# Sixteen output tensors, one for each batch and channel half, in place of one

## The chip, the cores and the metric

The kernel runs on one core of a Trainium2 chip. The metric is device time in microseconds (us), from the start to the end of one execution; less is better. A core has five engines with a queue each: PE (matrix multiply), DVE (vector), ACT (scalar), POOL (GpSimd) and SP, which issues transfers. An engine works its queue strictly in order. A transfer (DMA) runs on its own once it is issued; whoever needs its result, or the memory that it reads, waits on a semaphore that it raises when it has landed. Here SP issues all plain transfers and POOL all indirect ones (gathers and scatters of rows by a list of indices).

## What is computed

For each of 8 batches x[b] of 3136 tokens with 256 channels, the kernel filters along the tokens in the frequency domain. It then picks the 128 tokens with the largest score against a gate vector, and adds to these a gated feed-forward result; all other tokens stay as the filter left them.

```python
X = np.fft.rfft(x, axis=1)
y = np.fft.irfft(X * (filt_r + 1j * filt_i)[None], n=3136, axis=1)
scores = np.einsum('bsd,d->bs', y, w_gate)
out = y.copy()
for b in range(8):
    top = np.argpartition(-scores[b], 128)[:128]
    xe = y[b, top]
    ye = np.maximum(xe @ w1, 0.0) @ w2            # 256 -> 1024 -> 256
    out[b, top] = xe + sigmoid(scores[b, top])[:, None] * ye
```

## The kernel before

The filter of a batch is a transform of two factors (98 x 32), a product with the filter, and the way back. `outer` runs the first and last stage over 8 chunks of 32 channels: it takes batch b_out out and brings batch b_in in at the same time. `inner` does the middle stage. The way out of a chunk ends in matmuls (`imm`, L531), copies from PSUM by ACT into a tile `xh` and into `X` (`iout`, L537) and an addition and a subtraction by POOL or DVE (`join`, L541). `xh` has four buffers, so ACT's copy for a chunk waits until the joins four chunks earlier are done.

`X` holds one batch in two channel halves. When the four chunks of a half x are done, `store_rows` (L577, issued by SP) writes the half to the output in DRAM, 2 MB at a time: 16 stores in all. The output is one tensor, `out_0_dram`, of 8 batches x 8192 rows of 128 channels; rows 0 to 4095 of a batch are its first channel half, the next 4096 its second.

`select` finds the 128 tokens of a batch by counting against thresholds and ends in `c12`: it writes two columns of row numbers to `idx_sb`, one for each half (L867, L868). The number includes the batch's offset, which L637 adds. `ffn` then takes the batches in the groups [0], [1], [2, 3, 4], [5, 6] and [7]: `gather` (L962) fetches the 128 rows, one indirect DMA for each half; PE transposes them (L968), multiplies with w1 (L991 or L998) and w2 (L1026 or L1031); `gated` (L1034, DVE) adds the result to the gathered rows; `scatter` (L1039) writes them back, again one indirect DMA for each half. The batches 0 and 1 use the tile `xr`, the others rows of `fb_sb`.

The order of all instructions is fixed: the steps are recorded and run in the order of the list `ORDER`, so each engine's queue is written by hand. What an instruction waits for isn't written by hand. The framework finds it from the tiles and DRAM ranges that the instruction reads and writes, and places the waits. Gathers and scatters give it a range of the output, not rows, since the rows are known only at run time: `of[:(b + 1) * ROWS]`, the whole output from its start to the end of batch b. The DMAs that POOL issues take eight semaphores in turn (DMASW0 to DMASW7 in the rows below), so each also waits for the one that used its semaphore before, eight issues earlier.

## Time and profile before

| | us |
|---|---|
| median of 3 runs | 461.66 (460.04 to 465.23) |
| the profiled execution | 465.2 |
| its span, first to last instruction | 463.4 |

| engine | busy us | share of the span |
|---|---|---|
| PE | 412.6 | 89% |
| DVE | 362.4 | 78% |
| POOL | 344.1 | 74% |
| ACT | 313.4 | 68% |

The profile gives, for one execution, when each instruction ran, how long its engine sat idle just before it, and which event ended that idle time. The releaser is inferred from semaphores: where an instruction waits for several, the one named is the one that came last by the profile, and a name that had long been done stands for another, often a DMA. A DMA that POOL issues shows as busy time of POOL while its descriptors are made; the data lands later. PEclk is the granted clock of PE as a share of full speed, 2.4 GHz; its lower level is 1.2 GHz.

### The profile page before, as it was taken

Reading aid. Unit: us, or ns where it says so; the run is one execution under the profiler, and the core shown is the slowest. Engines: PE = TensorE matmul, PEld = TensorE weight load, DVE = VectorE, ACT = ScalarE, POOL = GpSimd, SP = SyncE. Lnnn points to the kernel's source line nnn. Section 1 sums busy time; section 2 is a strip of 40 time slices with the busy share of each in tenths; the row PEclk is TensorE's granted clock in tenths of the full one; section 3 lists DMA queues with packets and bytes.
Section 4 is the critical chain, followed back from the end, with each engine's and each line's share of the span. In section 5 each row is a group of like instructions: output and inputs, shape, how many; then the busy total and the mean of one; then the engine's idle time right before and its main releaser. Section 6 shows DMA issues by size and latency. Waiting matters only on the chain.

```text
span 463.4 us, 13106 instructions
## 1 busy us (share of the span) xinstructions
PE 412.6 (89%) x5348; PEld 246.1 (53%) x5348; DVE 362.4 (78%) x727; ACT 313.4 (68%) x798; POOL 344.1 (74%) x231
## 2 busy tenths in 40 slices
PE   9999999999799999998999999999999895988710
PEld 9645555445545554465545444554567552877700
DVE  3668999989888989996799999989999984552300
ACT  1719866997578898877797977799899774421100
POOL 3218989799797968899989884998899959452332
PEclk9999999999899999999999999999999997999965
DMA  8899441174627464555445466424264340441000
GB/s 286 269 327 345 178 185 38 70 296 185 219 92 274 182 219 192 199 190 213 182 184 223 180 230 272 168 101 180 95 229 181 119 194 23 171 154 63 24 23 23
DMA packets 12554, 80.82 MB, mean 174 GB/s; under 512 B 3150, under 2 KB 6222, under 8 KB 7886
## 3 DMA queue, kind: packets, MB, share of 16 engines
q1 hardware_dynamic: 11470, 77.89, 44.9%
q0 software_dynamic: 1024, 2.10, 1.5%
q8 instruction: 42, 0.69, 0.6%
q14 instruction: 18, 0.15, 0.1%
HBM read 45.20 MB, written 34.78 MB: 173 GB/s over the span
## 4 chain that ended last, share of the span: by engine, by line
PE 39%; DVE 28%; ACT 12%; POOL 9%; issue 8%; DMA 3%; POOLq 0%; ACTq 0%; DVEq 0%
DVE t L479 6%; DVE UU L505 5%; DVE y L384 5%; ACT junk L441 5%; DVE q L391 4%; PE pv L998 3%; PE py L500 3%; DMA out_dram<-fb_sb,idx_sb 3%; PE pa L500 3%; PE pv L500 2%; POOL q L435 2%; PE py L400 2%; PE pa L376 2%; ACT junk L716 2%; PE pv L400 2%
## 5 line engine op out<-in xcount | busy, mean ns | idle before, releaser
L435 POOL TENSOR_TENSOR q<-UU,wg_sb 128x1024 f32<-128x1024 f32 (+1 forms) x47 | 110.2, 2352 | 12.7 <-ACT UU L408 6.3
L541 POOL TENSOR_TENSOR X<-xh,X 113x512 f32<-113x512 f32 x64 | 82.0, 1292 | 13.4 <-ACT X L537 9.4
L441 ACT ACTIVATE junk<-q 128x256 bf16<-128x256 f32 x180 | 75.1, 417 | 11.4 <-POOL q L435 6.5
L479 DVE STREAM_TRANSPOSE t<-UU 128x1024 f32<-128x1024 f32 x64 | 78.0, 1223 | 0.0
L387 POOL TENSOR_TENSOR q<-q,fb_sb 128x1024 f32<-128x1024 f32 (+1 forms) x18 | 40.7, 2262 | 11.6 <-ACT q L380 11.5
L489 POOL TENSOR_TENSOR X<-X 113x512 f32<-113x512 f32 x24 | 31.3, 1307 | 15.5 <-DVE xh L489 7.6
L489 POOL TENSOR_TENSOR xh<-X 113x512 f32<-113x512 f32 x26 | 33.5, 1297 | 6.5 <-DMA X<-in_x_dram 6.5
L716 ACT ACTIVATE junk<-R,nb 128x392 bf16<-128x392 f32 (+1 forms) x48 | 30.0, 625 | 6.6 <-DVE nb L737 6.0
L441 ACT ACTIVATION_READ_ACCUMULATOR junk<-q 128x1 f32 x180 | 33.9, 188 | 0.0
L500 PE MATMUL pa<-X,c_sb 49*64 49x512 f32 x192 | 30.3, 596 | 0.7 <-DVE UU L505 0.5
L500 PE MATMUL pv<-X,c_sb 49*64 49x512 f32 x184 | 29.7, 612 | 0.0
L505 DVE STREAM_TRANSPOSE UU<-pa 128x1024 f32<-128x1024 f32 x21 | 25.9, 1232 | 4.9 <-PE pa L500 4.8
L1039 POOL DMA_INDIRECT out_dram<-fb_sb,idx_sb x12 | 11.7, 973 | 24.2 <-DMA out_dram<-fb_sb,idx_sb 19.2
L505 DVE STREAM_TRANSPOSE UU<-pv 128x1024 f32<-128x1024 f32 x19 | 23.4, 1233 | 5.5 <-PE pv L500 5.3
L1010 ACT ACTIVATE q<-pv 128x384 fp32r<-128x384 f32 (+2 forms) x18 | 8.0, 457 | 29.1 <-PE pv L998 20.5
L1012 DVE SCALAR_TENSOR_TENSOR y<-pv,q 128x384 fp32r<-128x384 f32 (+2 forms) x18 | 9.0, 511 | 23.1 <-ACT q L1010 18.5
L384 DVE TENSOR_TENSOR y<-pa,fa_sb 128x1024 f32<-128x1024 f32 (+1 forms) x19 | 22.5, 1185 | 3.7 <-PE pa L376 1.5
L500 PE MATMUL py<-X,c_sb 49*64 49x512 f32 x168 | 23.9, 592 | 0.0
L376 PE MATMUL pa<-UU,tf_sb 64*64 64x256 f32 x292 | 21.8, 406 | 1.6 <-ACT X L567 0.5
L563 PE MATMUL pz<-t,c_sb 64*64 64x512 f32 x160 | 22.2, 595 | 0.1
L400 PE MATMUL py<-y,ti_sb 64*64 64x256 f32 x252 | 21.1, 380 | 0.6 <-DVE y L384 0.6
L400 PE MATMUL py<-q,ti_sb 64*64 64x256 f32 x252 | 20.9, 376 | 0.0
(342 smaller groups left out, 1167.8 us busy)
## 6 DMA issues: line engine op xcount, KB each, us to landing
out_dram<-X SPq DMA_DIRECT2D x16, 2048.0 KB, 6.8
X<-in_x_dram SPq DMA_DIRECT2D x14, 2048.0 KB, 8.6
X<-in_x_dram SPq DMA_DIRECT2D x4, 1024.0 KB, 12.9
R<-scr SPq DMA_DIRECT2D x14, 196.0 KB, 3.4
fb_sb<-in_moe_w_dram SPq DMA_DIRECT2D x2, 1024.0 KB
fa_sb<-in_fri_dram SPq DMA_DIRECT2D x4, 256.0 KB, 8.7
fb_sb<-in_fri_dram SPq DMA_DIRECT2D x4, 256.0 KB
ti_sb<-in_ti_dram SPq DMA_DIRECT2D x1, 576.0 KB, 10.2
```

Of the source, the lines that this page charges most:

```text
L376: nc.tensor.matmul(z[o, hi, e], lhsT=tf_sb[p, l], rhs=urow(b, l, 0, D)[p], start=True, stop=True)
L384: nc.vector.tensor_tensor(out=wide(y), in0=wide(h["z"]), in1=filt(fa_sb), op=ALU.mult)
L387: nc.gpsimd.tensor_tensor(out=wide(h["q"]), in0=wide(h["q"]), in1=filt(fb_sb), op=ALU.mult)
L400: nc.tensor.matmul(v[o, j, c], lhsT=ti_at[p, k, 2 * i + e, hi], rhs=y[p, hi, c], start=k == 0, stop=k == 1)
L435: nc.gpsimd.tensor_tensor(out=h["q"][:, e0:e0 + ne].rearrange("p e (j d) -> p e j d", j=2), in0=u.rearrange("p e d j -> p e j d"), in1=wg_ ...
L441: nc.scalar.activation(out=rk, in_=h["q"][:, e, j * D:j * D + D], func=AF.Copy, accum_out=urow(b, ls[2 * e + j], D, DS))
L479: nc.vector.transpose(out=h["t"].rearrange("p d (l j) -> p d l j", j=2), in_=uchan(b_out, c))
L489: eng.tensor_tensor(out=(area(1) if k else h["f"])[:64 + NH], in0=area(0)[:64 + NH], in1=area(1)[:64 + NH], op=(ALU.add, ALU.subtract)[k])
L500: nc.tensor.matmul(ap[64 * k:64 * k + 64, g].rearrange("p (n d) -> p n d", d=DW), lhsT=todo[k][i][0][p], rhs=todo[k][i][1][p], start=i == ...
L505: nc.vector.transpose(out=uchan(b_in, c), in_=a.rearrange("p (l j) d -> p d l j", j=2))
L541: eng.tensor_tensor(out=area(k)[:64 + NH], in0=h["e"][:64 + NH], in1=odd, op=(ALU.add, ALU.subtract)[k])
L716: nc.scalar.activation(out=junk, in_=st["R"][:, ph], func=AF.Sign, bias=st["nb"], accum_out=cnt)
```

## The change

The output becomes 16 DRAM tensors of 4096 rows, `yd[b][x]`, one for each batch and channel half; in the program they are `out_0_dram` to `out_15_dram`, with batch b in 2b and 2b + 1. A token's row number is now the same in both halves and has no batch offset, so `idx_sb` has one column for each batch: L868 falls away, and the addition of L637 becomes a copy. Stores, gathers and scatters name their own tensor. The host puts the tensors together by a reshape, as it did before. `ORDER` is the same.

```diff
--- before.py
+++ after.py
-ROWS = 8192
+ROWS = 4096
...
-    cst: bass.AP, wg: bass.AP, w1: bass.AP, w2: bass.AP, out: bass.AP, C: int,
+    cst: bass.AP, wg: bass.AP, w1: bass.AP, w2: bass.AP, yd: list, C: int,
...
-    of = out.rearrange("b s d -> (b s) d")
...
-    idx_sb = const.tile([128, 2 * B], I32, name="idx_sb")
+    idx_sb = const.tile([128, B], I32, name="idx_sb")
...
     def store_rows(b, x):
-        to = out[b, 4096 * x:4096 * x + 4096].rearrange("(p r) d -> p (r d)", p=128)
-        nc.sync.dma_start(out=to, in_=X[:, x].rearrange("p k n d -> p (k n d)"))
+        nc.sync.dma_start(out=yd[b][x].rearrange("(p r) d -> p (r d)", p=128), in_=X[:, x].rearrange("p k n d -> p (k n d)"))
...
-            nc.vector.tensor_scalar(out=Dt[:, 2 * N2:], in0=cc["row"][:N1], scalar1=float(b * ROWS), scalar2=None, op0=ALU.add)
+            nc.vector.tensor_copy(out=Dt[:, 2 * N2:], in_=cc["row"][:N1])
...
-            st["idx"] = idx = idx_sb[:, 2 * b:2 * b + 2]
+            st["idx"] = idx = idx_sb[:, b:b + 1]
...
-            nc.vector.tensor_scalar(out=idx[:C, 1:], in0=idx[:C, :1], scalar1=4096.0, scalar2=None, op0=ALU.add)
...
         def gather(j):
             for x in range(2):
-                nc.gpsimd.indirect_dma_start(out=xe[j][:C, x * HD:x * HD + HD], out_offset=None, in_=of[:(bs[j] + 1) * ROWS],
-                                             in_offset=bass.IndirectOffsetOnAxis(ap=sts[bs[j]]["idx"][:C, x:x + 1], axis=0))
+                nc.gpsimd.indirect_dma_start(out=xe[j][:C, x * HD:x * HD + HD], out_offset=None, in_=yd[bs[j]][x],
+                                             in_offset=bass.IndirectOffsetOnAxis(ap=sts[bs[j]]["idx"][:C, 0:1], axis=0))
...
         def scatter(j):
             for x in range(2):
-                nc.gpsimd.indirect_dma_start(out=of[:(bs[j] + 1) * ROWS],
-                                             out_offset=bass.IndirectOffsetOnAxis(ap=sts[bs[j]]["idx"][:C, x:x + 1], axis=0),
+                nc.gpsimd.indirect_dma_start(out=yd[bs[j]][x],
+                                             out_offset=bass.IndirectOffsetOnAxis(ap=sts[bs[j]]["idx"][:C, 0:1], axis=0),
                                              in_=xe[j][:C, x * HD:x * HD + HD], in_offset=None)
...
-    args.append(nc.dram_tensor("out_0_dram", (B, ROWS, D // 2), F32, kind="ExternalOutput").ap())
+    yd = [[nc.dram_tensor(f"out_{2 * b + x}_dram", (ROWS, D // 2), F32, kind="ExternalOutput").ap() for x in range(2)] for b in range(B)]
+    args.append(yd)
```

The instructions of PE, ACT and SP stand as before. On DVE eight instructions (L868) are gone. On POOL every instruction stands at its place, but their waits differ. Three places follow; a row is a line of the code, the operation, output<-input with buffer numbers, the size, and the semaphores that the instruction waits for (DMASW: DMAs issued by POOL; DMAHW: by SP; else an engine). Lines of the change lie 2 or 3 below those of before (L1036 is L1039, L959 is L962, L540 is L541, L930 is L933).

POOL, where it scatters batch 0, before:

```order
L933 TENSOR_TENSOR fa_sb_4718<-fb_sb_88,fa_sb_4718 128x512
L1039 DMA out_0_dram<-xr_97,idx_sb_91 8192x128 [waits DMASW4_49,DMASW5_49,DMASW3_49,DMASW6_49,DMASW2_49,DMASW7_49,DMASW1_49,DMASW0_49]
L1039 DMA out_0_dram<-xr_97,idx_sb_91 8192x128 [waits DMASW2_49]
L933 TENSOR_TENSOR ti_sb_4819<-fb_sb_88,ti_sb_4819 128x512 [waits PE_49,Activation_49]
L933 TENSOR_TENSOR fa_sb_4718<-fb_sb_88,fa_sb_4718 128x512 [waits Activation_49]
L541 TENSOR_TENSOR X_89<-xh_4964,X_89 113x16x32 [waits DMAHW4_49]
L541 TENSOR_TENSOR X_89<-xh_5055,X_89 113x16x32 [waits Activation_49]
L541 TENSOR_TENSOR X_89<-xh_4964,X_89 113x16x32 [waits Pool_49]
```

The same place in the change:

```order
L930 TENSOR_TENSOR fa_sb_4713<-fb_sb_88,fa_sb_4713 128x512
L1036 DMA out_0_dram<-xr_97,idx_sb_91 4096x128 [waits DMASW2_49]
L1036 DMA out_1_dram<-xr_97,idx_sb_91 4096x128 [waits DMASW3_49]
L930 TENSOR_TENSOR ti_sb_4813<-fb_sb_88,ti_sb_4813 128x512 [waits PE_49,Activation_49]
L930 TENSOR_TENSOR fa_sb_4713<-fb_sb_88,fa_sb_4713 128x512 [waits Activation_49]
L540 TENSOR_TENSOR X_89<-xh_4958,X_89 113x16x32 [waits DMAHW4_49]
L540 TENSOR_TENSOR X_89<-xh_5049,X_89 113x16x32 [waits Activation_49]
L540 TENSOR_TENSOR X_89<-xh_4958,X_89 113x16x32 [waits Pool_49]
```

Before, the first scatter waits for all eight DMAs last issued, and the second for DMASW2, which is the first. In the change the two write two tensors and wait only for the DMAs that used DMASW2 and DMASW3 eight issues earlier, the gathers of batch 1.

POOL, where it gathers batch 7, before:

```order
L541 TENSOR_TENSOR X_89<-xh_5186,X_89 113x16x32
L541 TENSOR_TENSOR X_89<-xh_5186,X_89 113x16x32 [waits Pool_49]
L541 TENSOR_TENSOR X_89<-xh_5228,X_89 113x16x32
L962 DMA fb_sb_88<-out_0_dram,idx_sb_91 128x128 [waits DMAHW6_49,DMAHW7_49,DVE_49,PE_49]
L962 DMA fb_sb_88<-out_0_dram,idx_sb_91 128x128 [waits DVE_49,PE_49]
```

The same place in the change:

```order
L540 TENSOR_TENSOR X_89<-xh_5180,X_89 113x16x32
L540 TENSOR_TENSOR X_89<-xh_5180,X_89 113x16x32 [waits Pool_49]
L540 TENSOR_TENSOR X_89<-xh_5221,X_89 113x16x32
L959 DMA fb_sb_88<-out_14_dram,idx_sb_91 128x128 [waits DMASW2_49,DMAHW6_49,DVE_49,PE_49]
L959 DMA fb_sb_88<-out_15_dram,idx_sb_91 128x128 [waits DMAHW7_49,DMASW3_49,PE_49]
```

Before, the first of the two gathers carries the waits for both stores of batch 7; in the change each waits for the store of its own half, and for a semaphore last used by the scatters of batch 0.

The end of POOL's queue, the scatters of batches 2 to 7, before:

```order
L1039 DMA out_0_dram<-fb_sb_88,idx_sb_91 24576x128 [waits DMASW3_49,DMASW2_49,DMASW6_49,DMASW1_49,DMASW7_49,DMASW0_49,DVE_49]
L1039 DMA out_0_dram<-fb_sb_88,idx_sb_91 24576x128 [waits DMASW4_49]
L1039 DMA out_0_dram<-fb_sb_88,idx_sb_91 32768x128 [waits DMASW5_49,DVE_49]
L1039 DMA out_0_dram<-fb_sb_88,idx_sb_91 32768x128 [waits DMASW6_49]
L1039 DMA out_0_dram<-fb_sb_88,idx_sb_91 40960x128 [waits DMASW7_49,DVE_49]
L1039 DMA out_0_dram<-fb_sb_88,idx_sb_91 40960x128 [waits DMASW0_49]
L1039 DMA out_0_dram<-fb_sb_88,idx_sb_91 49152x128 [waits DMASW1_49,DVE_49]
L1039 DMA out_0_dram<-fb_sb_88,idx_sb_91 49152x128 [waits DMASW2_49]
L1039 DMA out_0_dram<-fb_sb_88,idx_sb_91 57344x128 [waits DMASW3_49,DVE_49]
L1039 DMA out_0_dram<-fb_sb_88,idx_sb_91 57344x128 [waits DMASW4_49]
L1039 DMA out_0_dram<-fb_sb_88,idx_sb_91 65536x128 [waits DMASW5_49,DVE_49]
L1039 DMA out_0_dram<-fb_sb_88,idx_sb_91 65536x128 [waits DMASW6_49]
```

The same place in the change:

```order
L1036 DMA out_4_dram<-fb_sb_88,idx_sb_91 4096x128 [waits DMASW4_49,DVE_49]
L1036 DMA out_5_dram<-fb_sb_88,idx_sb_91 4096x128 [waits DMASW5_49]
L1036 DMA out_6_dram<-fb_sb_88,idx_sb_91 4096x128 [waits DMASW6_49,DVE_49]
L1036 DMA out_7_dram<-fb_sb_88,idx_sb_91 4096x128 [waits DMASW7_49]
L1036 DMA out_8_dram<-fb_sb_88,idx_sb_91 4096x128 [waits DMASW0_49,DVE_49]
L1036 DMA out_9_dram<-fb_sb_88,idx_sb_91 4096x128 [waits DMASW1_49]
L1036 DMA out_10_dram<-fb_sb_88,idx_sb_91 4096x128 [waits DMASW2_49,DVE_49]
L1036 DMA out_11_dram<-fb_sb_88,idx_sb_91 4096x128 [waits DMASW3_49]
L1036 DMA out_12_dram<-fb_sb_88,idx_sb_91 4096x128 [waits DMASW4_49,DVE_49]
L1036 DMA out_13_dram<-fb_sb_88,idx_sb_91 4096x128 [waits DMASW5_49]
L1036 DMA out_14_dram<-fb_sb_88,idx_sb_91 4096x128 [waits DMASW6_49,DVE_49]
L1036 DMA out_15_dram<-fb_sb_88,idx_sb_91 4096x128 [waits DMASW7_49]
```

Before, the first waits for the gathers, and each further one for the DMASW of the scatter just ahead of it, beside DVE (`gated`) for the first half of a batch. In the change each waits for the DMA eight issues earlier, and for DVE in the same places.

## Rows read from the trace of the kernel before

**Rows 1.** Span of the core and its granted clock (us; 1.0 is full clock):
```profile
core 0: 463.4 us, clock 0.964
```

**Rows 2.** Page, costliest groups: busy us, mean ns | idle before, its releaser:
```profile
L1039 POOL DMA_INDIRECT out_dram<-fb_sb,idx_sb x12 | 11.7, 973 | 24.2 <-DMA out_dram<-fb_sb,idx_sb 19.2
```

**Rows 3.** Timeline of POOL at the end: start, us, instruction [idle before <-releaser]:
```profile
439.08 0.97 POOL L1039 DMA_INDIRECT out_dram<-fb_sb,idx_sb  x1 [2.15 <-DVE fb_sb L1034]
456.68 0.97 POOL L1039 DMA_INDIRECT out_dram<-fb_sb,idx_sb  x1 [2.14 <-DMA out_dram<-fb_sb,idx_sb]
459.42 0.97 POOL L1039 DMA_INDIRECT out_dram<-fb_sb,idx_sb  x1 [1.78 <-DMA out_dram<-fb_sb,idx_sb]
```

**Rows 4.** Timeline of DVE: the last results of the feed-forward batches:
```profile
418.46 0.47 DVE L1034 SCALAR_TENSOR_TENSOR fb_sb<-pa,g_sb,fb_sb 128x256 f32<-128x256 f32 x1
438.35 0.48 DVE L1034 SCALAR_TENSOR_TENSOR fb_sb<-py,g_sb,fb_sb 128x256 f32<-128x256 f32 x1
441.53 0.48 DVE L1034 SCALAR_TENSOR_TENSOR fb_sb<-pa,g_sb,fb_sb 128x256 f32<-128x256 f32 x1 [2.11 <-PE pa L1031]
```

**Rows 5.** Line L1039 (scatters): us from a DMA's issue to its landing:
```profile
DMA to landing us min/median/max: 2.2/2.2/6.7
```

**Rows 6.** Line L962 (gathers): the same:
```profile
DMA to landing us min/median/max: 2.5/3.1/8.9
```

**Rows 7.** Timeline of POOL, scatters of batches 0 and 1:
```profile
373.10 1.01 POOL L1039 DMA_INDIRECT out_dram<-xr,idx_sb  x1 [0.16 <-issue]
379.38 0.98 POOL L1039 DMA_INDIRECT out_dram<-xr,idx_sb  x1 [5.27 <-PE py L727]
400.10 0.97 POOL L1039 DMA_INDIRECT out_dram<-xr,idx_sb  x1 [6.24 <-DMA out_dram<-xr,idx_sb]
```

**Rows 8.** Chain that ended last: start us, us, what:
```profile
382.91 3.65 POOL X L541 x3
```

**Rows 9.** Timeline of ACT, and of PE, after that:
```profile
386.59 0.59 ACT L537 COPY xh<-py 113x512 f32<-113x512 f32 x1 [5.36 <-POOL X L541]
387.72 0.50 PE L849 MATMUL pa<-Dt,rows 64*64 64x65 f32 x8 [5.25 <-ACT X L537]
```

**Rows 10.** Windows: busy us (xcount) PE PEld DVE ACT POOL, PEclk, DMA share, GB/s:
```profile
382.40:387.70 5.30, 0.07 (x6) 0.00 (x0) 0.97 (x4) 1.11 (x3) 5.30 (x5) 0.85 0.00 0
387.70:393.90 6.20, 6.18 (x42) 3.19 (x46) 4.27 (x16) 4.11 (x10) 6.00 (x6) 0.58 0.11 42
442.10:463.40 21.30, 0.00 (x0) 0.00 (x0) 0.00 (x0) 0.00 (x0) 6.50 (x7) 0.55 0.06 22
```

**Rows 11.** Timeline of PE: equal groups of matmuls before and after its idle time:
```profile
379.96 1.04 PE L531 MATMUL py<-t,c_sb 64*64 64x512 f32 x8
388.21 1.98 PE L531 MATMUL py<-t,c_sb 64*64 64x512 f32 x8
380.93 1.32 PE L998 MATMUL pv<-fa_sb 128*128 128x384 f32 x6
390.12 2.29 PE L998 MATMUL pv<-fa_sb 128*128 128x384 f32 x6
```

**Rows 12.** Timeline of POOL, gathers of batch 7:
```profile
422.26 0.96 POOL L962 DMA_INDIRECT fb_sb<-out_dram,idx_sb  x1 [9.53 <-DMA out_dram<-X]
423.52 0.94 POOL L962 DMA_INDIRECT fb_sb<-out_dram,idx_sb  x1 [0.30 <-issue]
```

**Rows 13.** Timeline of PE's weight loads: first transposes of batch 7:
```profile
426.25 0.14 PEld L968 LDWEIGHTS pz<-c_sb,fb_sb 128*128 128x128 f32 x1 [0.27 <-DMA fb_sb<-out_dram,idx_sb]
```

**Rows 14.** Timeline of DVE: the second index of batch 7:
```profile
416.04 0.15 DVE L868 TENSOR_SCALAR idx_sb<-idx_sb 128x1 int32<-128x1 int32 x1
```

**Rows 15.** Page, DMA issues: count, KB each, median us to landing:
```profile
out_dram<-X SPq DMA_DIRECT2D x16, 2048.0 KB, 6.8
X<-in_x_dram SPq DMA_DIRECT2D x14, 2048.0 KB, 8.6
X<-in_x_dram SPq DMA_DIRECT2D x4, 1024.0 KB, 12.9
```

## What the change is predicted to do

> **What bounds the kernel now.** I read the page first: PE is busy for most of the span, DVE, POOL and ACT for two thirds to three quarters, so no engine is the bound alone, and what counts is which wait ends last in each stretch. The page's costliest groups show one large idle time that isn't PE's: POOL sat idle for 24.2 us ahead of the twelve scatters of the batches 2 to 7, 19.2 of them until a scatter had landed [rows 2]. The chain that ended last shows where this counts: at its end it goes from scatter to scatter, of which the last starts at 459.42 [rows 3]. The windows say the same: from 442.1 to the end at 463.4 PE, DVE and ACT do nothing, and POOL is busy for 6.5 of 21.3 us, the DMA engines for 6% [rows 1, 10].
>
> The timeline of POOL shows the pattern. A scatter keeps POOL busy for 0.97 us, then POOL waits 1.78 or 2.14 us for its landing, then comes the next [rows 3]; a scatter takes 2.2 us from issue to landing [rows 5]. The results had long been there: batch 4's was done at 418.93, batch 6's at 438.83, and the last, batch 7's, at 441.53 + 0.48 = 442.01 [rows 4], but the last scatter started at 459.42 [rows 3].
>
> The same wait stands twice further up, where the batches 0 and 1 are written. There the second scatter waited 5.27 and 6.24 us [rows 7]. The releaser of the first is given as a matmul of PE, but the order shows that this scatter waits for DMASW2 alone, the scatter before it, which had started at 373.10: 379.38 - 373.10 = 6.28 us, near the longest landing of a scatter, 6.7 [rows 5]. What stands behind it in POOL's queue is wanted elsewhere: two parts of the weight split (L933), then the joins of batch 7. The first three joins ran until 382.91 + 3.65 = 386.56 [rows 8]; ACT sat idle for 5.36 us until then, because its next copy needs the `xh` buffer that they free, and PE sat idle for 5.25 us behind ACT [rows 9]. After that idle time the granted clock of PE was 0.58 over 387.7 to 393.9, so for the most part at the lower of its two levels, 1.2 in place of 2.4 GHz [rows 10]. Equal groups of matmuls took 1.98 in place of 1.04 us and 2.29 in place of 1.32 [rows 11].
>
> **The change part by part.** The waits between scatters, and between scatters and gathers, go. By the order each scatter now waits for DVE's result and for the DMA eight issues earlier. That one is long over: for batch 7's scatters it is batch 3's.
>
> *The end.* Batch 7's first scatter starts about 0.25 us behind its result, as batch 4's did behind a result that ended at 438.83 (439.08 - 438.83) [rows 3, 4]; so 442.01 + 0.25 = 442.26. The second follows at the step of two indirect DMAs that don't wait for each other, 423.52 - 422.26 = 1.26 us [rows 12]: 443.52. Before it was 459.42, so with the same end behind it the span is shorter by 15.9 us. For this POOL has to be through with the batches 2 to 6. It is free from 424.46 on, when batch 7's gathers are issued [rows 12], and batch 4's result is there by then. The eight scatters of 2 to 5 take 8 x 1.26 = 10.1 us of the 14.4 until batch 6's result at 438.83, and batch 6's pair is issued by 438.83 + 0.25 + 1.26 + 0.97 = 441.3 [rows 3, 4, 12], ahead of batch 7's. POOL's issuing isn't the bound.
>
> No row shows two scatters in flight. The nearest is gathers in a row, 2.5 to 3.1 us to landing [rows 6] against 2.2 [rows 5]; the last scatter lands between 0 and 0.9 us later than now. I take 0, since the last pair runs with nothing else in flight. At the far end stands the 6.7 us of [rows 5], which is a rival below. The Trainium skill, page "DMA: Bandwidth & Descriptors", section "Rules for kernel authors", speaks against splitting: two transfers of halves run on the same 16 engines and take turns. Here the DMA engines were busy for 6% of 21.3 us for seven scatters [rows 10], so 0.18 us for one; by the rule the second half might land up to that much later, and the sum would be 22.9 in place of 23.1 us. The rows have no say on it, since none has a pair in flight.
>
> *The middle.* Batch 0's second scatter starts at 373.10 + 1.26 = 374.36 in place of 379.38, so POOL is 5.0 us earlier with the joins, and ACT's copy at 386.59 comes 5.0 us earlier, at 381.6. ACT was free at 386.59 - 5.36 = 381.2 and PE at 387.72 - 5.25 = 382.5, so nothing else holds them there, and PE's idle 5.25 us shrinks to about 0.2 [rows 9]. If nothing further down waits for what doesn't move, all up to batch 7's result moves by 5.0. What is outside that chain: the gathers of the batches 5 and 6 and the store that batch 7's gather needs move up too, with the joins, and by more, as batch 1's second scatter no longer waits 6.24 us [rows 7]. I give that second wait no gain of its own, as PE wasn't waiting for POOL there.
>
> *The clock.* Without the idle time PE's clock should stay at the full level. Of the groups of [rows 11] that saves 0.94 + 0.97 = 1.9 us. The bounds are 0 (something else holds PE there) and 1.9; I take 1.9, as PE was busy for 6.18 of 6.20 us in that window [rows 10], so it was its own bound.
>
> *Batch 7's gathers.* Each waits only for its own half's store, so both can be done by the time when now the second starts. PE waited 0.27 us for them [rows 13]; that goes.
>
> *DVE.* Eight instructions such as L868 go, 0.15 us each [rows 14], 1.2 us in all; the copy for L637 is the same size. They overlap their neighbours, so from 0 to 1.2; I take 0.
>
> *The stores.* Same bytes, same place in SP's queue. No row shows tensors of their own, so I take 0; what a slower store would cost is a rival.
>
> The sum is 15.9 + 5.0 + 1.9 + 0.3 = 23.1 us. The profiled execution took 465.2 us for a span of 463.4, so 442.1 us and a span of 440.3 after. It was the slow end of the three runs; from their median, 461.66, it is 438.6 us, and that is the forecast.
>
> **The rivals.**
>
> *Only the end is gained.* The 5.0 us in the middle go, but PE or ACT meets its next wait: the joins of batch 7 go on behind the three, and ACT's later copies wait for these; or the steps from 400 to 441, in which PE, ACT and DVE hand each other short pieces, hang on something that I haven't moved. For it: POOL was busy for all of the 5.3 us in which PE sat idle, and for 6.00 of the 6.20 behind them [rows 10], so it may well be the bound there with its joins. Against: the joins themselves move by 5.0. Then 15.9 us are left, 445.8 us from the median.
>
> *Late landing.* More DMAs in flight land later, as batch 0's first scatter did, beside a store: 6.7 in place of 2.2 us [rows 5], so 4.5 us given back at the end, 443.1 us. Against: all stores have landed by then. The Trainium skill, the same page, section "Latency and other measured facts", gives HBM's access as ten times longer under load; by that the landing would follow the load, and the trace agrees, 2.2 us in the quiet end against 6.7 beside a store.
>
> *One at a time all the same.* POOL can't make a second list of descriptors while the first is in use, so scatters stay 2.75 to 3.1 us apart [rows 3], in the middle too: nothing changes, 461 us. Against: gathers follow each other at 1.26 us [rows 12] with landings of 3.1 [rows 6], so two or three are in flight.
>
> *The stores get slower,* the case on the other side. A load of a next batch into `X` waits for the store of the half that it overwrites, and there are 14 loads of a half. A store lands in 6.8 us; a load of the same size takes 8.6, and loads at the busy start take 12.9 [rows 15]. If all 14 waits lay on the path, 23.1 / 14 = 1.65 us a store would use up the gain, and from 2.0 us on the kernel would be over 1% slower; at 8.6 it is 438.6 + 14 x 1.8 = 463.8 us, at 12.9 it is 438.6 + 14 x 6.1 = 524.0. Against: a half was one run of 2 MB before, too, and its pieces are the same.
>
> **How the numbers follow.** The forecast with all four terms has 0.72; it lies between 435 (460.04, the fastest run, less 23.1 and 1.2) and 442 (the profiled execution's own). Only the end: 0.15. Late landing: 0.05. One at a time: 0.04. Slower stores: 0.02. Some other small gain: 0.02. The range goes from 435 to 446 and takes in the second and third case. A measurement of this kernel can tell about 1%, or 4.6 us, from no change. One at a time is within that, slower stores split between within and slower: faster 0.94, same 0.04, slower 0.02.
>
> **What would show it.** The last scatter starts 1.2 to 1.3 us after the one before it, and about 1.5 us after batch 7's `gated`; idle time ahead of the scatters names DVE, not a DMA. Near 374 the second scatter of batch 0 follows at 1.26 us. ACT has no 5 us of idle time at the copy that now stands at 386.59, PE none of 5 us at L849, and the granted clock stays near 1 in the stretch after it. Batch 7's `gated` ends near 442.0 - 7.2 = 434.8. If it ends near 442, only the end was gained. Were the stores slower, their landing would be above 6.8 us. The forecast is wrong if scatters still wait for each other's landing, or if DVE's results come later than now.

## The result, and the profile after

The kernel with sixteen tensors took 446.54 us (median; 445.49 to 449.43) where the kernel before took 462.1 us (460.04 to 465.23): a ratio of 0.967 with a 95% interval of 0.960 to 0.974. The forecast was 438.6 us with a range of 435 to 446. So it is faster, by 15.6 us by the medians in place of 23.1, and just outside the range. The profiled execution took 446.96 us for a span of 444.7. Lines of the kernel after are three lower than before at these places: scatters L1036, gathers L959, `gated` L1031; the joins are one lower, L540.

The end is nearly as forecast. The page's group of scatters, the span, and the timeline of POOL (start, us, instruction, [idle before it <- what ended that]):

```profile
core 0: 444.7 us, clock 0.992
```
```profile
L1036 POOL DMA_INDIRECT out_dram<-fb_sb,idx_sb x12 | 11.7, 973 | 16.1 <-DVE fb_sb L1031 12.5
```
```profile
372.83 1.02 POOL L1036 DMA_INDIRECT out_dram<-xr,idx_sb  x1 [0.17 <-issue]
374.15 0.98 POOL L1036 DMA_INDIRECT out_dram<-xr,idx_sb  x1 [0.30 <-issue]
...
439.79 0.96 POOL L1036 DMA_INDIRECT out_dram<-fb_sb,idx_sb  x1 [0.83 <-issue]
441.06 0.97 POOL L1036 DMA_INDIRECT out_dram<-fb_sb,idx_sb  x1 [0.30 <-issue]
```

No scatter waits for a landing any more: the idle time ahead of the group names DVE's result where [rows 2] named a DMA. The last pair follows at 1.27 us, the last scatter starts at 441.06 in place of 459.42 [rows 3], and the pair of batch 0 stands 1.32 us apart, not 6.28 [rows 7].

The results of the batches moved by less than they should. DVE's `gated` products, first of the kernel after (the batches 1, 4, 5 and 7), then two of before whose rows weren't shown:

```profile
380.15 0.48 DVE L1031 SCALAR_TENSOR_TENSOR xr<-pa,g_sb,xr 128x256 f32<-128x256 f32 x1 [0.36 <-PE pa L1023]
413.63 0.48 DVE L1031 SCALAR_TENSOR_TENSOR fb_sb<-pa,g_sb,fb_sb 128x256 f32<-128x256 f32 x1
430.36 0.48 DVE L1031 SCALAR_TENSOR_TENSOR fb_sb<-pa,g_sb,fb_sb 128x256 f32<-128x256 f32 x1 [0.96 <-PE pa L1028]
438.80 0.48 DVE L1031 SCALAR_TENSOR_TENSOR fb_sb<-pa,g_sb,fb_sb 128x256 f32<-128x256 f32 x1 [2.01 <-PE pa L1028]
```
```profile
378.47 0.48 DVE L1034 SCALAR_TENSOR_TENSOR xr<-pa,g_sb,xr 128x256 f32<-128x256 f32 x1 [0.36 <-PE pa L1026]
433.00 0.48 DVE L1034 SCALAR_TENSOR_TENSOR fb_sb<-pa,g_sb,fb_sb 128x256 f32<-128x256 f32 x1 [0.97 <-PE pa L1031]
```

With batch 0's first scatter, these marks and the last scatter cut the run into five stretches. They are used all through what follows, each as the difference of two starts, in us:

| | A: scatter 0 to gated 1 | B: to gated 4 | C: to gated 5 | D: to gated 7 | E: to last scatter |
|---|---|---|---|---|---|
| before | 5.37 | 39.99 | 14.54 | 8.53 | 17.89 |
| after | 7.32 | 33.48 | 16.73 | 8.44 | 2.26 |
| difference | +1.95 | -6.51 | +2.19 | -0.09 | -15.63 |

The start of A (-0.27) and what follows the last scatter (3.98 and 3.64) make up the rest of 463.4 - 444.7 = 18.7. So B and E gave nearly what the sum had given them (6.9 and 15.9), and A and C, which the sum did not mention, took 4.1 us back.

*Stretch B.* The windows of [rows 10], now (us, busy us of PE, PEld, DVE, ACT and POOL with counts, granted clock of PE, DMA share, GB/s), with one ahead of them, which is of 360.0 to 372.8, and the same place before:

```profile
360.00:372.80 12.80, 11.17 (x92) 6.57 (x84) 11.71 (x21) 8.67 (x24) 12.14 (x11) 0.87 0.30 105
382.40:387.70 5.30, 4.59 (x52) 2.89 (x52) 5.12 (x16) 4.56 (x12) 5.19 (x5) 1.00 0.00 0
387.70:393.90 6.20, 6.20 (x59) 4.35 (x53) 3.89 (x12) 3.90 (x10) 5.56 (x6) 1.00 0.87 354
```
```profile
360.00:373.10 13.10, 11.31 (x100) 7.37 (x92) 12.32 (x25) 10.50 (x27) 12.29 (x12) 1.00 0.29 103
```

PE's 5.25 idle us are gone, and the clock is 1.00 where it was 0.58. But the clock is 0.87 in the stretch ahead, where before had 1.00. That is (1 - 0.87) x 12.8 / 0.5 = 3.3 us at the lower level; the trace's own record of the clock has 3.4 us, from 368.9 on.

*Stretch A.* What differs there begins ahead of batch 0's scatter. DVE, POOL and PE of the kernel after, then the same of before:

```profile
361.64 4.80 DVE L930 TENSOR_TENSOR fa_sb<-fb_sb,fa_sb 128x512 fp32r<-128x512 f32 x1
367.27 3.02 DVE L669 TENSOR_TENSOR q<-kf,c_sb 98x416 f32<-98x416 f32 x2
...
362.16 1.28 POOL L930 TENSOR_TENSOR fa_sb<-fb_sb,fa_sb 128x512 fp32r<-128x512 f32 x1
...
367.32 0.30 PE L725 MATMUL pa<-c_sb,cnt 64*64 64x8 f32 x8 [0.74 <-DVE kf L656]
368.78 3.33 PE L676 MATMUL pv<-q,c_sb 104*128 104x416 f32 x4 [0.79 <-DVE q L669]
```
```profile
361.55 0.68 DVE L933 TENSOR_TENSOR fa_sb<-fb_sb,fa_sb 128x512 fp32r<-128x512 f32 x1
362.28 4.37 DVE L541 TENSOR_TENSOR X<-xh,X 113x512 f32<-113x512 f32 x1
367.17 2.17 DVE L671 TENSOR_TENSOR q<-kf,c_sb 98x416 f32<-98x416 f32 x2 [0.39 <-POOL q L668]
...
362.36 1.29 POOL L933 TENSOR_TENSOR fa_sb<-fb_sb,fa_sb 128x512 fp32r<-128x512 f32 x1
...
369.39 0.97 PE L678 MATMUL pv<-q,c_sb 104*128 104x416 f32 x2 [0.61 <-DVE q L671]
```

A product of DVE stands beside a product of POOL. Before, DVE's ended at 362.23 and POOL's began at 362.36. After, POOL's began 0.52 us behind DVE's start, and DVE's took 4.80 us where 0.68 is its own length. Before, it was DVE's next product, a join, that took 4.37 us. DVE's steps behind the late product are late, PE waits twice for them (0.74 and 0.79), and then ran at half its clock for 3.4 us: four matmuls that took 0.97 a pair took 3.33. The Trainium skill, page "SBUF — State Buffer", section "SBUF: two separate sides", says that DVE, with two inputs in SBUF, and POOL share one pair of ports, and that the one that starts first keeps it. The trace agrees that one stands still for the other; that it is the first that goes on, it doesn't: by the records DVE had started first. (In e1, e2 and e4 below POOL's started 0.2 us ahead, as the page has it, and DVE's took 4.1 us.)

*Stretch C.* ACT, DVE and PE of the kernel after, and the piece of the chain that ended last:

```profile
419.37 0.38 ACT L1007 ACTIVATE q<-pv 128x256 fp32r<-128x256 f32 x1 [1.17 <-issue]
423.58 0.38 ACT L1007 ACTIVATE q<-pv 128x256 fp32r<-128x256 f32 x1 [3.83 <-remote]
...
424.00 0.42 DVE L1009 SCALAR_TENSOR_TENSOR y<-pv,q 128x256 fp32r<-128x256 f32 x1 [5.34 <-ACT q L1007]
...
420.53 0.88 PE L995 MATMUL pv<-fa_sb 128*128 128x256 f32 x6
424.48 0.38 PE L1028 MATMUL py<-ti_sb,y 128*128 128x256 f32 x1 [2.73 <-DVE y L1009]
```
```profile
419.75 3.75 another core or an unknown queue
```

ACT's step at 423.58 waits for PE's six matmuls, which by their rows were done at 420.53 + 0.88 = 421.41. The trace shows PE's count of that semaphore at 423.50, 2.1 us later; ACT, then DVE, then PE waited for it, and PE stood idle for 2.73 us, until 424.48. Just ahead of that POOL was issuing six scatters (414.57 to 421.96) one behind the other. No row names what held the count back. That is what the experiments had to settle.

The rest is as forecast: stores and loads land as before.

```profile
out_dram<-X SPq DMA_DIRECT2D x16, 2048.0 KB, 6.7
X<-in_x_dram SPq DMA_DIRECT2D x14, 2048.0 KB, 8.7
```

For the scatters the trace of the kernel after gives no landing, as counts of their semaphores are missing in it. Its packets of the last scatter end 1.89 us behind the scatter's start (442.95 - 441.06), as before (461.31 - 459.42). The nearest landing is that of the kernel with two tensors below (e6), whose scatters overlap in pairs:

```profile
DMA to landing us min/median/max: 2.2/2.2/6.6
```

### The profile page after: what moved, and what is told of

The parts are those of the page before. It is cut to its first block, busy times and chain, and to the rows that moved or that the text cites. A ratio compares the mean times of both kernels' runs of the same rounds, so it can differ in the third digit from the quotient of the medians.

```text
span 444.7 us, 13092 instructions
## 1 busy us (share of the span) xinstructions
PE 411.4 (93%) x5348; PEld 246.1 (55%) x5348; DVE 363.7 (82%) x719; ACT 313.5 (71%) x798; POOL 344.9 (78%) x231
## 4 chain that ended last, share of the span: by engine, by line
PE 42%; DVE 30%; ACT 13%; issue 9%; POOL 3%; another core or an unknown queue 1%; POOLq 0%; ACTq 0%; DVEq 0%
ACT junk L440 6%; DVE t L478 6%; DVE UU L504 6%; DVE y L383 5%; DVE q L390 4%; PE py L499 3%; PE pa L499 3%; PE pv L399 3%; PE pv L499 3%; PE py L1107 2%; ACT junk L714 2%; PE pa L375 2%; PE py L399 2%; PE pz L399 2%; PE pa L1023 2%
## 5 line engine op out<-in xcount | busy, mean ns | idle before, releaser
L540 POOL TENSOR_TENSOR X<-xh,X 113x512 f32<-113x512 f32 x64 | 82.7, 1303 | 13.4 <-ACT X L536 9.2
L499 PE MATMUL pv<-X,c_sb 49*64 49x512 f32 x184 | 28.8, 594 | 0.0
L1036 POOL DMA_INDIRECT out_dram<-fb_sb,idx_sb x12 | 11.7, 973 | 16.1 <-DVE fb_sb L1031 12.5
L959 POOL DMA_INDIRECT fb_sb<-out_dram,idx_sb x12 | 11.5, 955 | 12.6 <-PE pv L995 9.9
```

The source lines that it names most:

```text
L499: nc.tensor.matmul(ap[64 * k:64 * k + 64, g].rearrange("p (n d) -> p n d", d=DW), lhsT=todo[k][i][0][p], rhs=todo[k][i][1][p], start=i == ...
L540: eng.tensor_tensor(out=area(k)[:64 + NH], in0=h["e"][:64 + NH], in1=odd, op=(ALU.add, ALU.subtract)[k])
```

## The experiments

Fourteen kernels, in the order in which they ran. All but e7, which is the kernel before itself, are written from one source, in which a table says for batch `b` and half `x` in which tensor and from which row on it lies; their lines are 16 higher than those after the change at the scatters (L1052) and at `gated` (L1047), and less further up. Where two halves of a batch start at different rows, the second index (L868 before) is there for it. Gathers and scatters see a tensor up to their own batch's rows, as in the kernel before. The diffs give the table as a formula. The stretches of all of them are from one profile each; the ratios are of all executions:

| | A | B | C | D | E | ratio to before, interval |
|---|---|---|---|---|---|---|
| e1 sixteen again | 8.97 | 33.51 | 18.43 | 8.53 | 2.26 | 0.9668, 0.9640 to 0.9695 |
| e2 end only | 8.91 | 35.77 | 16.07 | 8.50 | 2.27 | 0.9729, 0.9691 to 0.9767 |
| e3 middle only | 8.86 | 33.56 | 14.55 | 8.50 | 12.45 | 0.9836, 0.9798 to 0.9874 |
| e4 eight | 6.60 | 38.20 | 14.55 | 8.49 | 7.58 | 0.9743, 0.9708 to 0.9777 |
| e5 chain of 2 to 4 | 6.32 | 33.70 | 14.57 | 8.49 | 2.27 | 0.9542, 0.9506 to 0.9577 |
| e6 two | 5.37 | 33.43 | 14.54 | 8.53 | 2.27 | 0.9529, 0.9494 to 0.9565 |
| e7 before again | 5.37 | 39.65 | 14.57 | 8.49 | 18.12 | |
| e8 three | 7.59 | 33.65 | 17.74 | 8.50 | 2.27 | 0.9706, 0.9667 to 0.9745 |
| e9 four | 7.67 | 33.48 | 17.93 | 8.50 | 2.27 | 0.9691, 0.9656 to 0.9725 |
| e10 sixteen, step moved | 5.37 | 33.67 | 17.90 | 8.49 | 2.27 | 0.9652, 0.9625 to 0.9680 |
| e11 two, step moved | 5.36 | 33.78 | 14.56 | 8.50 | 2.27 | 0.9557, 0.9530 to 0.9583 |
| e12 breaks between pairs | 5.37 | 33.80 | 14.77 | 8.50 | 2.27 | 0.9571, 0.9519 to 0.9623 |
| e13 one break late | 5.37 | 33.91 | 17.72 | 8.49 | 2.27 | 0.9636, 0.9585 to 0.9688 |
| e14 one break ahead | 5.36 | 33.91 | 17.09 | 8.52 | 2.28 | 0.9613, 0.9557 to 0.9668 |

**e1, the change once more.** No edit but the table.

```diff
+PLACE[b][x] = (tensor 2*b + x, row 0)
```

> The changed kernel once more (its 16 tensors written by a table), to get a second profile and a better median. Known from its first profile: TensorE at half level 368.9 to 372.3 us (about 1.7 us dearer than the kernel before at the same steps) and ScalarE's relu at 423.58 waiting 3.83 us for TensorE (about 2.1 us dearer). Theory T1 (both losses are a matter of the single execution): at least one of them is gone or at another place in the new profile, and the runs spread over more than 1%, with the fastest at 442 to 444 us. Theory T2 (both come with the change, from the new order of work): both stand within 0.5 us of the same steps, median 445 to 448, spread under 1%.

Median 448.52 us (446.57 to 448.97). Both losses stand in the same stretches, and larger: 8.97 and 18.43 us; the one in C came 4 us earlier, at ACT's step at 419.52. That step, and windows over the two places:

```profile
419.52 0.38 ACT L1023 ACTIVATE q<-pv 128x256 fp32r<-128x256 f32 x1 [4.19 <-remote]
```
```profile
368.50:375.30 6.80, 6.38 (x28) 4.01 (x28) 4.41 (x12) 3.18 (x9) 6.31 (x6) 0.50 0.71 296
419.70:426.50 6.80, 5.72 (x25) 5.43 (x26) 0.85 (x2) 0.98 (x3) 1.95 (x2) 0.50 0.09 29
```

PE ran at half clock in both. So in this execution the lower level came with the idle time in C, and C cost 3.9 us where the first profile, which had no half-level stretch there, shows 2.2. T1 falls, except that the size and, in C, the place vary; the median is 0.5 us above T2's range.

**e2, the end alone, and e3, the middle alone.**

```diff
-PLACE[b][x] = (tensor 2*b + x, row 0)
+e2: (tensor 0, row (2*b + x) * 4096) for b < 2, else (tensor 2*b + x - 3, row 0)
+e3: (tensor 2*b + x, row 0) for b < 2, else (tensor 4, row (2*(b - 2) + x) * 4096)
```

> Batches 0 and 1 share one tensor (so their four scatters wait for each other again), batches 2 to 7 keep two tensors each: the end of the change without its middle. The prediction's sum (the middle is worth 5.0 + 1.9 + 0.3 us): DVE's 5.3 us wait of POOL's second scatter is back, 446.5 + 7.2 = 453.7 us. Theory T3 (the middle is worth only the 2.7 us that the first profile shows net): 449.2 us. Theory T4 (the middle gains nothing that lasts, the 2.7 are noise): 446 to 447.5 us.

> Batches 0 and 1 have two tensors each, batches 2 to 7 share one, so that the twelve last scatters wait for each other again. The prediction's sum (end worth 15.9): 462.1 - 7.2 = 454.9 us; T3 (middle worth 2.7): 459.4 us; T4 (middle worth nothing): 461 to 463 us. In all of them the last scatter starts about 18 us after the last gated product of batch 7.

e2 took 450.59 us, 12.6 us less than before by its ratio; e3 455.21, 7.6 us less. So the middle is worth 7.6 us alone, but only 2.8 us on top of the end. The stretches say why the two don't add up. e3's scatters still go one by one (its last three):

```profile
442.10 0.97 POOL L1052 DMA_INDIRECT out_dram<-fb_sb,idx_sb  x1 [1.76 <-DMA out_dram<-fb_sb,idx_sb]
445.22 0.97 POOL L1052 DMA_INDIRECT out_dram<-fb_sb,idx_sb  x1 [2.15 <-DMA out_dram<-fb_sb,idx_sb]
447.96 0.97 POOL L1052 DMA_INDIRECT out_dram<-fb_sb,idx_sb  x1 [1.77 <-DMA out_dram<-fb_sb,idx_sb]
```

Its chain of twelve takes 447.96 - 415.81 = 32.15 us, as before (459.42 - 427.32 = 32.10), but started 11.5 us earlier, behind batch 7's gathers; so E shrank to 12.45 with the waits in place. And C is 14.55 in e3, with its scatters one by one, but 16.07 in e2, where six stood in a row. So e3's time is that of the prediction's sum (454.9), but not for the sum's reason, as all the theories had E at 18 us; e2 lies between T3 and the sum, nearest to T3. (The interval of e3's ratio lies below 1, but its gain is less than 2%.)

**e4, eight tensors.**

```diff
+PLACE[b][x] = (tensor b, row x * 4096)
```

> One tensor for each batch, eight in all: only the second half's scatter waits, for the first half's of its own batch. Batches are free of each other, so the chain of twelve waits becomes three short pairs at the end. Worked from the first profile of the change: pairs of about 4.4 us (1 us issue, 2.3 us landing, 1 us issue) for batches 2 to 4 hide before batch 5's product at 430.4; batch 6's pair ends about 440.5, batch 7's second scatter starts at about 443.8 instead of 441.1, +2.7 us; the middle's first wait is back: +2.7 (T3) to +7.2 us (the sum). 452 to 456.5 us. If instead each second scatter waits as long as the slow 6.7 us landing, +7 at the end and 456 to 461 us.

451.76 us, just below the range. A second half waits for the first of its own batch, as expected: 1.76 or 1.77 us five times of six, and 3.56 once; E is 7.58, C 14.55. B is 38.20, as batch 0's second scatter waits again (4.80 us). A has the long product (4.08 us) but no half-level stretch, and is 6.60: so the late product alone costs 1.2 us, and the clock up to 2.4 more. In e2 and e4, where batch 0's second scatter still waits, A is longer and B shorter than before, and the two together are 44.68 and 44.80 us against 45.36: what A loses there comes out of that wait.

**e5 and e6, scatters in a row taken apart; e7, before again.**

```diff
-PLACE[b][x] = (tensor 2*b + x, row 0)
+e5: tensor 4 and row (2*(b - 2) + x) * 4096 for b = 2, 3, 4; all others a tensor each
+e6: (tensor x, row b * 4096)
```

> Only batches 2, 3 and 4 share a tensor, so that their six scatters wait for each other (a start every 3.2 us or so, in place of every 1.27 us); batches 0, 1, 5, 6 and 7 keep two tensors each. Theory B1 (TensorE's stall between batch 4's and batch 5's gated products comes from six scatters issued back to back beside it): the stretch from batch 4's gated product to batch 5's is 14.5 to 14.6 us as in the kernels whose scatters wait (before, e3, e4), not 16.7 and 18.4 as with sixteen tensors; the six scatters end about 432.5, so batch 5's start about 2 us after its product, batch 7's as early as before: the median goes down by 2 to 4 us to 443 to 446 us, ratio 0.958 to 0.964. Theory B2 (the stall is the clock's, from what TensorE did earlier): the stretch stays 16 to 18.5 us and the time 447 to 449 us.

> Two tensors, one for each channel half: a scatter waits for the one before it of its own half, two ahead of it on the queue, so that two are in flight at a time in place of one (before) or as many as fit (sixteen). By the landing of 2.2 us a wait of about 1 us stands ahead of every second scatter: six of batches 2 to 4 take about 10 us in place of 7.4, all hidden; batch 0's second scatter doesn't wait for its first. The end gains what sixteen tensors gain, to 0.3 us. B1: with the scatters in pairs TensorE's stall is smaller than with sixteen or gone, 444 to 448 us, ratio 0.960 to 0.968. B2: as sixteen, 447 to 449 us. If batch 0's and 1's second scatters still wait for something else of their half, 450 to 452 us.

> The kernel before once more, for a second profile of it. If TensorE's half-level stretch at 367 to 370 us (in four of the five kernels with more tensors) is a matter of the execution, it can stand here too, or the dip at 386 us can be gone; if it comes with the change, the clock falls again only after the wait for ScalarE at 382 to 388 us, and from batch 0's first scatter to batch 1's gated product it is 5.4 us again.

e5 442.37 us, e6 442.31: some 6 us better than sixteen tensors, with fewer waits taken away. POOL and ACT of e6:

```profile
413.08 1.00 POOL L1052 DMA_INDIRECT out_dram<-fb_sb,idx_sb  x1 [1.10 <-DVE y L1025]
414.43 1.00 POOL L1052 DMA_INDIRECT out_dram<-fb_sb,idx_sb  x1 [0.35 <-issue]
416.22 0.97 POOL L1052 DMA_INDIRECT out_dram<-fb_sb,idx_sb  x1 [0.79 <-DVE y L1025]
417.49 0.97 POOL L1052 DMA_INDIRECT out_dram<-fb_sb,idx_sb  x1 [0.30 <-issue]
...
416.55 0.39 ACT L1023 ACTIVATE q<-pv 128x256 fp32r<-128x256 f32 x1 [1.17 <-PE pv L1011]
418.74 0.38 ACT L1023 ACTIVATE q<-pv 128x256 fp32r<-128x256 f32 x1 [1.80 <-PE pv L1011]
```

The wait ahead of every second scatter is 0.79 or 0.86 us in place of 0.30, the six take 8.5 in place of 7.4 us, and ACT's step waits 1.80 us for PE where it had waited 3.83. C is 14.54, as in the kernel before. B1 holds, B2 falls. Both came out below the range that I gave B1. In the profiles that is A: DVE's product was short in both, and A is 6.32 and 5.37. e7 gives before's stretches within 0.35 us (464.21 us), without a half-level stretch in A: so the loss in C is not a matter of the execution, but comes and goes with the row of scatters.

**e8 and e9, three and four in turn.**

```diff
+PLACE[b][x] = (tensor 4 + (2*(b - 2) + x) % k, row (2*(b - 2) + x) // k * 4096) for b = 2, 3, 4, k = 3 and 4
```

> Batches 2 to 4 share three tensors in turn, so that three of their six scatters are in flight at a time; all others have two tensors each. With the landing of 2.2 us and an issue of 1.27 us the third still waits a little or not at all. If TensorE's stall needs more than two in flight, it is here: 16 to 18.5 us from batch 4's gated product to batch 5's, ratio 0.962 to 0.968. If it needs all six free of waits, 14.5 us and 0.953 to 0.957.

> The same with four tensors: four in flight, by the landing of 2.2 us no scatter waits, so POOL issues the six back to back as with sixteen tensors, though four semaphores' worth of them can be open. If the back-to-back issue is what stalls TensorE: 16 to 18.5 us from batch 4's gated product to batch 5's and ratio 0.962 to 0.968. If it is the number of separate tensors: 14.5 us and 0.953 to 0.957.

448.64 and 447.7 us, C 17.74 and 17.93; both ratios lie above the range that I gave (0.962 to 0.968), and A is 7.6 and 7.7. With three tensors no scatter waited any more (starts at 413.82, 415.13, 416.43, 417.70), so both are rows without a break, and the row of ACT is that of the change again (e9):

```profile
422.28 0.39 ACT L1023 ACTIVATE q<-pv 128x256 fp32r<-128x256 f32 x1 [3.83 <-remote]
```

**e10 and e11, DVE's product out of POOL's way.** The step with DVE's product (`wlo`, number 1512 of the order) goes ahead of the one with the sum of the spectrum (1443), with sixteen and with two tensors.

```diff
+ORDER.remove(1512)
+ORDER.insert(ORDER.index(1443), 1512)
```

> Sixteen tensors, and one step of VectorE moved five places ahead: the product that stood beside POOL's at 361.6 us (4.1 to 4.8 us long in the four profiles where POOL had started first or within its 0.7 us, 0.68 in the four where it was done before) now stands ahead of the sum of the spectrum, done at about 360. Theory A1 (this collision delays the select of batch 7 by about 1 us and brings TensorE's waits of 0.7 and 0.8 us and the half-level stretch behind them): 0.68 us long, the waits ahead of TensorE's products of q are 0.2 and 0.6, from batch 0's first scatter to batch 1's gated product 5.4 to 6.3 us in place of 7.3 and 9.0, median 445 to 447 us against 448.5, ratio 0.957 to 0.964; TensorE's stall beside the six scatters stays. A2 (the collision costs nothing that lasts): ratio 0.965 to 0.969.

> Two tensors and the same step moved. With two tensors the profile had the product at 0.68 us already, so A1 expects little: the same first mode in every execution, 441 to 442.5 us and a ratio of 0.950 to 0.954, with the slow single run of 445 us gone. If the moved step delays the select by its own 0.7 us, 443 us and 0.955.

DVE of e10:

```profile
359.83 0.68 DVE L939 TENSOR_TENSOR fa_sb<-fb_sb,fa_sb 128x512 fp32r<-128x512 f32 x1
361.82 4.16 DVE L543 TENSOR_TENSOR X<-xh,X 113x512 f32<-113x512 f32 x1 [0.24 <-ACT X L539]
366.50 2.17 DVE L676 TENSOR_TENSOR q<-kf,c_sb 98x416 f32<-98x416 f32 x2 [0.39 <-POOL q L673]
```

The product has its own 0.68 us, DVE's next one with two inputs takes the blocked time in its stead, as in the kernel before, and A is 5.37, with no half-level stretch there. In the profile that is 2.0 to 3.6 us less than with sixteen tensors and the step in its place. The time shows much less of it: 446.33 us, a ratio of 0.9652 against 0.9668, with intervals that overlap; A1's range for the ratio (0.957 to 0.964) is missed and A2's (0.965 to 0.969) hit, and it stays open how often the late product stood in the timed executions. With two tensors, where the product was short already, nothing is gained: 442.33 us, 0.9557 against 0.9529, just above the range of 0.950 to 0.954. Of the stretches of these two kernels, which ran in one session, only C differs clearly (17.90 and 14.56), and their times lie 4.0 us apart.

**e12 to e14, a break without a wait.** As e10; POOL writes a small tile of its own twice at one or two places of the row.

```diff
+nc.gpsimd.memset(idle_sb, 0.0)   # twice
+e12: behind batch 2's and behind batch 3's scatters
+e13: behind batch 3's scatters;  e14: ahead of batch 2's scatters
```

> As e10 (sixteen tensors, the product moved), and POOL fills 8x256 numbers of a tile of its own twice behind batch 2's and behind batch 3's scatters: about 0.6 us of other work where the kernel with two tensors waits 0.5 us. Nothing waits for a landing. Theory P1 (it is POOL's eight indirect transfers in one unbroken row that go with TensorE's stall, and any break of it helps): 14.5 to 14.6 us from batch 4's gated product to batch 5's, ratio 0.953 to 0.958. Theory P2 (the shared tensor's wait for the landing is what helps): the stall stays, 16.7 to 18 us, ratio 0.963 to 0.968.

> As e12 with one break only, behind batch 3's scatters: a row of six (two gathers of batch 7, four scatters), the break, and two more, then batch 5's wait. Under P1 with a row of eight needed, the stall is gone: 14.5 us, ratio 0.953 to 0.958. If a row of six is enough, it stays: 16.7 to 18 us, 0.963 to 0.968. P2: it stays.

> As e12 with one break only, ahead of batch 2's first scatter: two gathers, the break, then six scatters in a row. Under P1 with a row of eight needed: 14.5 us, ratio 0.953 to 0.958. If six in a row are enough: 16.7 to 18 us, 0.963 to 0.968. In e2, whose two gathers stood 1.3 us ahead of the six scatters, the stretch was 16.1, so I expect the stall to stay.

e12 took 442.74 us, C 14.77. POOL and ACT of e12 (lines one higher again):

```profile
413.84 0.99 POOL L1053 DMA_INDIRECT out_dram<-fb_sb,idx_sb  x1 [0.30 <-issue]
414.82 0.66 POOL L1058 MEMSET idle_sb<- 8x256 f32 x2
416.02 0.97 POOL L1053 DMA_INDIRECT out_dram<-fb_sb,idx_sb  x1 [0.54 <-issue]
...
419.58 0.38 ACT L1024 ACTIVATE q<-pv 128x256 fp32r<-128x256 f32 x1 [1.80 <-PE pv L1012]
```

So 0.66 us of other work on POOL, with 0.54 us of idle time behind it, does what the wait for the landing did. P1 holds, P2 falls. In e13 (445.09 us, C 17.72) and e14 (444.9 us, C 17.09) PE has its idle time again:

```profile
417.06 0.62 PE L1012 MATMUL pv<-fa_sb 128*128 128x256 f32 x3 [2.60 <-issue]
```
```profile
422.50 0.38 PE L1045 MATMUL py<-ti_sb,y 128*128 128x256 f32 x1 [2.02 <-issue]
```

So one break isn't enough: with two gathers and four scatters ahead of it (e13), or six scatters behind it (e14), the loss stands. By the profile, that is; e14's ratio (0.961) is below the range for it, and its interval overlaps that of e12.

## Why the prediction was right and wrong

- **The end, 15.9.** Right: E fell by 15.63 us. The pair at 1.26 us and POOL's being through with the other batches held; what followed the last scatter was 3.64 us after and 3.98 before. The 0.25 us behind DVE's result did not: batch 7's first scatter started 0.51 us behind it (439.79 against 438.80 + 0.48), and that is nearly all of the 0.27 us by which E fell short. The prediction had read the 0.25 from a scatter of batch 4, which by the order waited for the scatter ahead of it and not for batch 6's result at 438.83; its 2.15 us of waiting are those of the other first halves [rows 3].
- **The middle and the clock, 5.0 + 1.9.** Right in its own stretch: B fell by 6.51 us, and by 6.1 to 6.6 in all twelve kernels in which batch 0's second scatter is free (after, e1, e3, e5, e6, e8 to e14). PE's 5.25 idle us went, and ACT's 5.36 with them; the granted clock is 1.00 where it was 0.58.
- **The step that failed** stands behind that term: "If nothing further down waits for what doesn't move, all up to batch 7's result moves by 5.0." I took "further down" as waits for things that stay, and looked for none that the change makes new. Batch 7's `gated` ended at 439.28, where I had named 434.8: 2.19 of these 4.5 us are C, 1.95 are A, and the rest is the middle and its neighbours (6.51 in place of 7.2, less the 0.27 and 0.09 of the start and D). Of the 7.5 us between 23.1 and 15.6, the two profiled executions show 4.8 (465.23 - 446.96 = 18.27); the other 2.7 us come from where these two lay among the timed ones, 3.1 us above the median before and 0.4 after. All rows were read from that slow execution of the kernel before, and the sum was taken off the median.
- **C is the change's own cost.** The prediction looked at what a row of free scatters does to POOL ("POOL's issuing isn't the bound") and to landings, not at what it does to the engines beside it. Eight profiles have a row of at least four scatters without a break (after, e1, e2, e8, e9, e10, e13, e14): C is 16.1 to 18.4 us. In the eight others, with a wait or other work behind every second scatter at the latest (before, e3 to e7, e11, e12), it is 14.5 to 14.8. In time, e10 and e11, which differ clearly in C alone, are 4.0 us apart. That the row does it is shown, in executions as they were recorded; how, is not. Nor is the part of the recording settled. The trace before has 395 counts of PE's semaphore, two more than the 393 instructions that raise it; in the first profile of the change it has 391. The Trainium skill, page "NOTIFIC — the notification-queue block", section "Overflow: three behaviours, one of which stalls the engine", says that the block which writes a trace's records can hold an engine up, or drop records, when a queue is full. Records were lost here; but e11 and e12 lost some too (390 each) and have no stall. All eight profiles with the row lost some (390 to 392), and those that lost at most one count of PE, ACT and DVE (before, e5, e6, e7) have no such row: so no run tells whether the row stalls PE where nothing is lost, or not recorded.
- **A is not of the change's making by any step that I can show.** It begins at 361.64, 11 us ahead of the first scatter that is freed. Before, DVE's product was through 0.13 us ahead of POOL's; after, and in e1 to e4, e8 and e9, it wasn't; in e5, e6 and e7 it was. With the late product (4.1 to 4.8 us) A is 6.6 where no half-level stretch follows (e4), 7.3 to 7.7 where one of 3.4 us does (after, e8, e9) and 8.9 to 9.0 where one of 6.8 us does (e1 to e3); without it A is 5.4, or 6.3 with a half-level stretch of 3.4 us (e5). So in A a few tenths of a microsecond further up decide. What moves them is open; but the seven profiles with the late product are just those, of the eleven with the step in its place, that lost counts of PE, ACT and DVE (9 to 21 of them), while before, e5, e6 and e7 lost none or one. So here too the recording may have a part, or the chip: e5, e6 and e7 ran together on one that none of e1 to e4 and e8 to e14 ran on. What A's loss is worth in the median is open, too: e10 took it away and gained 0.7 us by the ratios, with an interval that includes none.
- **The clock term** had one more fault: taking away PE's 5.25 idle us took away one half-level stretch of 6.8 us, but the lower level came back in A, mostly behind idle times of 0.7 to 0.8 us, and in C behind 2.0 to 2.7 us. In A such idle times don't decide it: e4 has them and kept the full level, e5 has only 0.5 and 0.6 us and fell. I had forecast that the lower level goes, and not asked where it could come up next.
- **The rivals.** "Only the end is gained" came nearest in its number, 445.8 us, and is wrong in its place: B was gained, and e2, whose edit frees the end alone, took 450.59. Late landing is out (the last scatter's packets end after 1.89 us as before, and in e6 a scatter lands in 2.2 us as in [rows 5]; the 6.7 us that this rival gave to batch 0's first scatter are those of batch 1's, and batch 0's had landed in 5.8, both beside a store), one at a time is out (1.27 us), slower stores are out (6.7 and 8.7 us against 6.8 and 8.6, [rows 15]). DVE's and the gathers' terms, 0 and 0.3, are too small to tell.
- **The sum as such** is what a kernel gets that keeps the gains and drops the row: with two tensors B and E fell by 6.56 and 15.62 us, A and C stood at 5.37 and 14.54, and the ratio of 0.953 is 439.9 us when it is applied to the 461.66 that the forecast started from.

## What to carry to other kernels

When a wait goes, ask what the instructions that it held apart do to the engines beside them once they run in a row: here four to six scatters behind each other went with a stretch that is 1.5 to 4 us longer, in which PE stood idle, and letting each wait for the last but one, or putting 0.66 us of other work between the pairs, gave that back and kept all of the gain. With the step moved in both, two tensors (442.33 us) beat sixteen (446.33 us) because they leave a wait that is hidden and breaks the row. And cut the run at marks that both kernels have: the stretches told the two gains from the two losses, where the end-to-end time showed only a sum that was two thirds of the forecast.

## What the runs showed of the hardware

- A row of four or six scatters on POOL, 1.27 us apart, went with a count of PE's semaphore that came 1.4 to 2.1 us behind the end of its matmul, and with 2.0 to 2.7 us of idle PE, in eight of eight profiles (all of which lost records). Pairs that start 0.5 us (e6, e11) or 0.9 us (e12) later than in the row did not.
- Behind that idle time PE ran at half its clock for 3.4 or 6.8 us in six of the eight profiles that have it (e1, e8, e9, e10, e13, e14; C 17.1 to 18.4 us), and at the full level in two (after, e2; C 16.7 and 16.1).
- A product of DVE with both inputs in SBUF that by the records started 0.52 us ahead of one of POOL's took 4.80 us in place of 0.68; it was the one that had started first that stood still, over three products of POOL in a row (362.16 to 365.88).
